# Attention and two MLPs on one core: operand differences issued ahead of their halves, six weight sums taken from the converted words, and the first block's inputs on ScalarE's DMA queue

## The chip, the cores and the metric

The kernel runs on one core of one Trainium2 chip. The metric is the device time of one execution in microseconds (us). The kernel before takes 918.45 us, the median of 3 runs (918.18 to 919.23). The engines are named PE (TensorE), DVE (VectorE), ACT (ScalarE), POOL (GpSimd) and SP (SyncE, which before the change issues every transfer).

## The reference

Attention with a causal window of 128 and a linear bias, then two MLPs with squared ReLU, all in float32:

```python
# q, k, v: 4 batches, 8 heads, 576 positions, 64 columns
scores = np.where(mask, scale * np.matmul(q, k.transpose(0, 1, 3, 2)) + bias[None], -1000000000.0)
attn = softmax(scores)                      # mask: 0 <= i - j < 128
x = matmul(attn, v)                         # as 2304 tokens x 512
x = (s * np.maximum(x @ w_in1, 0.0) ** 2 + b) @ w_out1
out = np.maximum(x @ w_in2, 0.0) ** 2 @ w_out2
# w_in: 512 x 2048, w_out: 2048 x 512
```

## The kernel before, in words

**Accuracy.** Every operand of a float32 product is split into a high and a low half of a shorter type, and each product is the sum of three: high by high, high by low, low by high. A split is two instructions: ACT copies the operand into the short type (the high half), and DVE subtracts that from the operand (the low half). The low half therefore waits for ACT, on DVE.

**Fewer products.** Both MLPs multiply blocks of 2 by 2 in seven products instead of eight. That needs sums and differences of blocks: of the weights (done once, kept in DRAM as halves and loaded where they are needed), of the inputs (`difference`, L957, then `halve_input`, L984), and in the second MLP's second layer of the activations.

**Weights.** They arrive as 64-bit words that are converted on ACT, DVE and POOL. For the second MLP's `w_out` the pair k has words in tiles `raws[(k, r)]`, r = 2 and 3. Before, the converted words of these two rows of blocks are stored to DRAM (`store_words`, tokens `x`) and loaded again later (`load_words`, tokens `y`, into new tiles r = 4 and 5), and from those `second_sums` (tokens `N`, two for each pair) makes four combinations, `second_sum_halves` (`R`) splits them, and `store_second_sums` (`t`) writes them to DRAM (L872 to L940). Pairs 0 and 1 use other buffers, the eight pairs are otherwise alike.

**Order.** The whole program is a list of some 2,460 tokens in one string, `ORDER` (L37 on). Each token calls one function of a table (L1220 for the steps of the last stage), and the class `InOrder` (L19) keeps every engine's instructions in the order in which the functions issue them. All rows of the profile therefore have line L29. Two more tables say which engine takes an instruction that several could take (`UNIT_ENGINES`, `CHOICE`: `N1.1:v` puts that sum on DVE, without an entry it goes to POOL).

**Stages.** From 0 to about 400 us attention and the first MLP run interleaved, in units of 256 positions. The last 64 positions of each sequence are the *tail*: eight small units (`tail_unit`, L450 on), whose last step, `places`, copies an attention output with ACT and writes it to DRAM (`xd` in the profile). The first block of the second MLP starts with `load_input` (L943): four tiles `yf`, two transfers each, from these writes; the differences `t1s`, `yt` and two in place; the halves `m2xh`, `m2xl` and so on. While this happens PE finishes the last groups of the first MLP, whose operands are `ga_62h`, `ga_62l`, `ga_63h`, `ga_63l` and whose products are in `oa`.

The second MLP has four blocks of tokens, n = 0 to 3. For n = 0 and 1 first and second layer are interleaved. For n = 2 and 3 the first layer's results of all eight pairs are kept in SBUF, and the second layer is done product by product: for each of the kinds m = 1, 2, 7, 6, 5, 4, 3, and for each pair, a weight is loaded (token `e`, `load_second`), the operand is made (`g`, `second_operand`, L1044), and nine matmuls follow (`X`, `second_product`, into `q`). The operand of m = 7 is a difference of two results, put into `r_all`; that of m = 6 takes two instructions, that of m = 3 one, and the other kinds use a result as it is:

```python
if m == 7:
    tt(src, a11, a21, ALU.subtract)
elif m == 6:
    tt(a21, a21, a22, ALU.add)
    tt(a11, a21, a11, ALU.subtract)
elif m == 3:
    tt(a12, a12, a11, ALU.subtract)
split(*operand_halves(n, e), src, act_copy, dve_sub)
```

So on DVE the difference and the low half of the same operand stand next to each other, with ACT's copy between them in time.

Of the kernel before, what the change touches and what calls it, by code (L numbers as in the profile page):

```python
# [11 lines left out]
U32 = mybir.dt.uint32  # L12
# [3 lines left out]
P = 128  # L16


class InOrder:  # L19
# [24 lines left out]
    H13 c21 L15 c20 M12 c22 C10 U10 G14 a23 H14 X10 l30 G15 M13 L16 S11 M14 b23 L17 G16 P11 D13 L18 T11 H15 c23 M15 H16
    C11 G17 l32 a30 G18 U11 H17 X11 H18 L19 G19 b30 L20 S12 M16 L21 k0.1 a32 l31 M17 M18 P12 T12 a31 H19 G20 c30 C12 H20
    L22 l33 G21 b32 U12 X12 L23 G22 H21 S13 L24 M19 a33 b31 M20 M21 H22 P13 l34 b33 T13 G23 C13 c31 a34 M22 H23 U13 L25
    c33 G24 G25 c32 L26 k3.0 D14 L27 H24 M23 H25 X13 D15 S14 G26 G27 M24 l35 b34 L28 L29 P14 k4.1 T14 M25 H26 a35 C14
    H27 c34 k4.0 G29 b35 U14 M26 D16 X14 G28 H28 S15 L30 c35 P15 M27 M28 T15 C15 D17 G30 L31 H29 G31 U15 X15 L32 S16 M29
    H30 H31 D18 G32 L33 P16 T16 M30 D19 C16 H32 G33 M31 M32 H33 S17 U16 L34 P17 T17 X16 G34 C17 M33 L35 H34 S18 U17 M34
    G35 X17 H35 P18 L36 D20 T18 G36 C18 M35 D21 S19 U18 L37 H36 P19 T19 X18 M36 C19 S20 D22 U19 G37 L38 H37 P20 M37 T20  # L50
    G38 X19 C20 L39 S21 U20 H38 G39 H39 L40 P21 M38 G40 L41 M39 D23 H40 T21 G41 L42 X20 H41 C21 k6.0 S22 U21 M40 k0.0
    P22 T22 X21 C22 M41 S23 U22 G42 D24 H42 k7.0 k1.1 L43 P23 T23 X22 M42 C23 S24 G43 H43 k3.1 U23 P24 L44 T24 D25 D26
    C24 X23 M43 k1.0 G44 H44 L45 G45 S25 U24 L46 D27 M44 k5.0 X24 P25 T25 H45 G46 k2.1 C25 H46 D28 L47 n0.0 n0.1 S26 U25
# [1218 lines left out]
```

## Time and profile before

| | |
|---|---|
| median of 3 runs | 918.45 us (918.18 to 919.23) |
| the profiled execution | 916.52 us, its span 914.7 us |
| PE busy | 878.5 us, 96% of the span |
| DVE busy | 663.4 us, 73% |
| ACT busy | 536.7 us, 59% |
| POOL busy | 167.7 us, 18% |
| transfers | 216.83 MB, mean 237 GB/s |
| chain of work that ended last | PE 81%, DVE 9%, ACT 4%, DMA 3% |

The span is the time from the first instruction to the last. The profiled execution is one more execution, 1.9 us below the median of the others. A share of busy time is an average over stages that differ much, so the table says only that PE is the engine that is nearly always at work; where it is not, the windows and the waits tell.

### The profile page before, as it was taken

Reading aid. Unit: us, or ns where it says so; the run is one execution under the profiler, and the core shown is the slowest. Engines: PE = TensorE matmul, PEld = TensorE weight load, DVE = VectorE, ACT = ScalarE, POOL = GpSimd, SP = SyncE. Lnnn points to the kernel's source line nnn. Section 1 sums busy time; section 2 is a strip of 40 time slices with the busy share of each in tenths; the row PEclk is TensorE's granted clock in tenths of the full one; section 3 lists DMA queues with packets and bytes.
Section 4 is the critical chain, followed back from the end, with each engine's and each line's share of the span. In section 5 each row is a group of like instructions: output and inputs, shape, how many; then the busy total and the mean of one; then the engine's idle time right before and its main releaser. Section 6 shows DMA issues by size and latency. Waiting matters only on the chain.

```text
span 914.7 us, 16299 instructions
## 1 busy us (share of the span) xinstructions
PE 878.5 (96%) x5680; PEld 787.4 (86%) x5680; DVE 663.4 (73%) x1504; ACT 536.7 (59%) x1227; POOL 167.7 (18%) x242
## 2 busy tenths in 40 slices
PE   5899999999999999989999999999999989999988
PEld 3789998878777777769999998888999989999988
DVE  7998885554558788865565866897969968448775
ACT  7888776454546677754454555666655635446442
POOL 4333221000024454200200122222213200000000
PEclk9899999999999999999999999999999999999999
DMA  9553636126337978988679766887999987876683
GB/s 344 174 190 99 201 112 195 47 70 219 103 100 242 313 248 271 307 305 316 226 287 355 262 229 198 306 294 261 319 336 349 327 282 252 292 265 229 187 271 98
DMA packets 131378, 216.83 MB, mean 237 GB/s; under 512 B 15840, under 2 KB 74208, under 8 KB 131296
## 3 DMA queue, kind: packets, MB, share of 16 engines
q1 hardware_dynamic: 131296, 215.79, 70.0%
q8 instruction: 45, 0.74, 0.3%
q14 instruction: 37, 0.30, 0.1%
HBM read 146.02 MB, written 69.73 MB: 236 GB/s over the span
## 4 chain that ended last, share of the span: by engine, by line
PE 81%; DVE 9%; ACT 4%; DMA 3%; issue 2%; SPq 1%; POOL 0%; ACTq 0%; DVEq 0%
PE ha L29 14%; PE po L29 14%; PE px L29 13%; PE oa L29 12%; PE py L29 10%; PE q L29 8%; PE s L29 7%; PE u L29 2%; DMA m2wol<-wd 1%; DVE ywoh L29 1%; DVE st L29 1%; DVE m2woh L29 1%; DVE pr_t L29 1%; DMA yf<-xd 1%; DMA st<-w_out 1%
## 5 line engine op out<-in xcount | busy, mean ns | idle before, releaser
L29 POOL TENSOR_TENSOR st<-st 128x256 int32<-128x256 int32 (+1 forms) x123 | 87.2, 729 | 363.8 <-DVE st L29 251.0
L29 ACT ACTIVATE pr<-pr,nd 128x256 f32<-128x256 f32 (+1 forms) x125 | 57.9, 474 | 49.5 <-DVE nd L29 49.5
L29 ACT ACTIVATE st<-st 128x512 int32<-128x512 uint32 (+3 forms) x74 | 62.4, 859 | 5.6 <-DVE st L29 3.4
L29 DVE SCALAR_TENSOR_TENSOR r_all<-r_all,s_sb 128x256 f32<-128x256 f32 (+1 forms) x64 | 43.0, 675 | 24.4 <-ACT r_all L29 23.8
L29 ACT ACTIVATE tr<-tr 128x384 f32<-128x384 f32 x48 | 25.2, 525 | 55.4 <-DVE tr L29 55.3
L29 PE MATMUL oa<-ga,woh 128*128 128x256 f32 x256 | 48.2, 287 | 0.0
L29 ACT ACTIVATE r_all<-ha 128x256 f32<-128x256 f32 (+1 forms) x64 | 31.0, 486 | 24.7 <-PE ha L29 19.2
L29 DVE SCALAR_TENSOR_TENSOR st<-st 128x512 int32<-128x512 int32 (+1 forms) x42 | 37.3, 890 | 11.0 <-ACT st L29 10.4
L29 PEld LDWEIGHTS oa<-ga,woh 128*128 128x128 f32 x256 | 39.7, 191 | 2.2 <-issue 1.8
L29 DVE CUSTOM_DVE_ANT_0 pr<-s,bases 128x256 f32<-128x256 f32 (+1 forms) x96 | 31.7, 385 | 11.3 <-PE s L29 11.3
L29 PE MATMUL ha<-x0h,wih 128*128 128x256 f32 x128 | 38.4, 300 | 0.0
L29 PE MATMUL ha<-x0l,wih 128*128 128x256 f32 x128 | 36.6, 286 | 0.0
L29 PE MATMUL ha<-x0h,wil 128*128 128x256 f32 x128 | 36.6, 286 | 0.0
L29 PE MATMUL oa<-ga,wol 128*128 128x256 f32 x128 | 36.2, 283 | 0.0
L29 POOL TENSOR_TENSOR sph<-wih,wil 128x256 f32<-128x256 f32 x17 | 13.5, 814 | 117.7 <-PE ha L29 117.2
L29 ACT ACTIVATE r_all<-px 128x384 f32<-128x384 f32 x32 | 15.7, 490 | 29.5 <-PE px L29 29.4
L29 PE MATMUL s<-raw 64*128 64x256 f32 (+1 forms) x224 | 30.5, 388 | 0.8 <-DVE x0l L29 0.8
L29 DVE TENSOR_SCALAR st<-st 128x512 int32<-128x512 int32 (+2 forms) x52 | 26.2, 507 | 5.9 <-ACT st L29 5.1
L29 POOL TENSOR_TENSOR sph<-sph 128x256 f32<-128x256 f32 x26 | 22.6, 888 | 33.7 <-DVE spl L29 20.9
L29 PE MATMUL px<-m2xl,m2wil 128*128 128x384 f32 x138 | 27.9, 337 | 0.0
L29 PEld LDWEIGHTS ha<-x0h,wih 128*128 128x128 f32 x128 | 24.9, 195 | 3.5 <-issue 2.5
L29 PE MATMUL ha<-x2h,wih 128*128 128x512 f32 x64 | 26.4, 412 | 0.0
(681 smaller groups left out, 2765.9 us busy)
## 6 DMA issues: line engine op xcount, KB each, us to landing
m2wih<-wd SPq DMA_DIRECT2D x19, 512.0 KB, 6.5
st<-w_in SPq DMA_DIRECT2D x8, 1024.0 KB, 6.0
st<-w_out SPq DMA_DIRECT2D x16, 512.0 KB, 5.0
ws<-spl SPq DMA_DIRECT2D x16, 512.0 KB, 4.2
m2wih<-ws SPq DMA_DIRECT2D x16, 512.0 KB, 6.1
wd<-m2wol SPq DMA_DIRECT2D x14, 512.0 KB, 4.5
m2wol<-we SPq DMA_DIRECT2D x26, 256.0 KB, 4.4
st<-w_out SPq DMA_DIRECT2D x6, 1024.0 KB, 6.9
```

The lines of the kernel that those rows point to most:

```text
L29: ins = op(*args, **kw)
```

## The change

Four things change.

1. `second_operand` is cut in two. `second_difference` (token `q`) has the subtractions of m = 7, 6 and 3, and stands in `ORDER` ahead of the token `g`, which now only splits. For m = 7 the differences go alternately into two buffers (`r_all` and `tu`).
2. For the pairs 2, 3 and 4 (`AT_ONCE`) the second sums are made from the converted words' own tiles; `ORDER` has no `x` and `y` for them any more, which is 6 stores and 6 loads of 256 KB, and their `N`, `R` and `t` stand earlier.
3. The eight writes of the tail's results, and the eight transfers of `load_input` for the first block, are issued by ACT instead of SP.
4. `ORDER`, `UNIT_ENGINES` and `CHOICE` are new as a whole. The built program has the same 5,248 matmuls; DVE has 1,524 instructions instead of 1,506, POOL 232 instead of 247, ACT 1,080 activations instead of 1,082 and 16 transfers, SP 690 transfers instead of 718. Of the sums of 128x256, POOL has 15 fewer and DVE 17 more.

```diff
...
-    X3.41 X3.42 X3.43 g3.48 X3.44 e3.45 e3.51 e3.48 X3.45 X3.46 O3.5.2 g3.49 X3.48.2 g3.47 X3.49.2 X3.50.2 X3.51.2
...
+    X3.39 e3.48 e3.45 X3.40 X3.41 X3.42 e3.54 X3.43 e3.47 X3.44 X3.45 g3.48 e3.51 e3.55 q3.51 e3.53 O3.5.2 q3.53 g3.46
...
-    N1.1:v N2.1:v N3.0:v N3.1:v N7.1:v S0.1:g S1.1:g S2.0:g S3.0:g S3.1:g S4.0:g b0.0:vg b2.2:vg b3.0:vg b3.1:vg
...
+    N0.1:v N1.0:v N3.0:v N4.0:v N4.1:v N5.1:v N6.1:v S0.0:g S0.1:g S1.0:g S1.1:g S3.1:g b0.0:vg b0.2:vg b2.0:vg
...
-EARLY, SOONER = 3, 2
+EARLY, SOONER, AT_ONCE = 3, 2, (2, 3, 4)
...
-            sync.dma_start(x_dram[LAST][:, 2 * hq:2 * hq + 2, cols], y.rearrange("p (y t) -> p y t", y=2))
+            scalar.dma_start(x_dram[LAST][:, 2 * hq:2 * hq + 2, cols], y.rearrange("p (y t) -> p y t", y=2))
...
-        return raws[(k, r)][:, h * DM:(h + 1) * DM]
+        return raws[(k, r - 2 if r > 3 and k in AT_ONCE else r)][:, h * DM:(h + 1) * DM]
...
     def load_input(n, q):
+        queue = sync if n else scalar
...
-            sync.dma_start(y[:, :, :BLK], a0[:, c, :])
-            sync.dma_start(y[:, :, BLK:], a1[:, c, :P])
+            queue.dma_start(y[:, :, :BLK], a0[:, c, :])
+            queue.dma_start(y[:, :, BLK:], a1[:, c, :P])
...
-    def second_operand(n, e):
+    def parts_of(n, e):
         m, y = SECOND[e // NP], e % NP
         a11, a22, a12, a21 = (result_of(n * NP + y, c) for c in range(4))
+        return m, a11, a22, a12, a21, {1: a11, 2: a12, 7: temp(f"u{3 + y % 2}"), 6: a11, 5: a21, 4: a22, 3: a12}[m]
+
+    def second_difference(n, e):
+        m, a11, a22, a12, a21, src = parts_of(n, e)
         tt = vector.tensor_tensor
-        src = {1: a11, 2: a12, 7: temp("u3"), 6: a11, 5: a21, 4: a22, 3: a12}[m]
         if m == 7:
             tt(src, a11, a21, ALU.subtract)
         elif m == 6:
...
         elif m == 3:
             tt(a12, a12, a11, ALU.subtract)
-        split(*operand_halves(n, e), src, act_copy, dve_sub)
+
+    def second_operand(n, e):
+        split(*operand_halves(n, e), parts_of(n, e)[-1], act_copy, dve_sub)
...
```

**The order on DVE in the last stage (n = 3), kinds m7 and m6.** `r_all` (and `tu` after the change) is the difference of an m7 operand, a tile that begins with `m2w` the half that is made from it; `yw..` are the first layer's results. Before:

```order
L29 TENSOR_TENSOR r_all<-ywol_7370 128x384
L29 TENSOR_TENSOR m2wil_4703<-r_all,m2wil_4703 128x384
L29 TENSOR_TENSOR ob_9148<-q_8982,k3m 128x512
L29 TENSOR_TENSOR ob_9154<-q_8983,k3m 128x256
L29 TENSOR_TENSOR r_all<-ywol_7370,ywoh_7518 128x384
L29 TENSOR_TENSOR m2wil_4703<-r_all,m2wil_4703 128x384
```

After the change:

```order
L29 TENSOR_TENSOR tu_7116<-ywol_7372 128x384
L29 TENSOR_TENSOR ywoh_7222<-ywoh_7222,ywil_7115 128x384
L29 TENSOR_TENSOR ywil_7115<-ywoh_7222,ywil_7115 128x384
L29 TENSOR_TENSOR m2wil_4702<-tu_7116,m2wil_4702 128x384
L29 TENSOR_TENSOR m2woh_4723<-ywih_7029,m2woh_4723 128x384
L29 TENSOR_TENSOR r_all<-ywol_7372,ywoh_7512 128x384
L29 TENSOR_TENSOR tu_7116<-ywoh_7512,yr_7643 128x384
L29 TENSOR_TENSOR m2wih_4481<-ywoh_7222,m2wih_4481 128x384
```

Between a difference and the half made from it now stand two or more other instructions.

**The order on ACT where the first MLP ends and the second MLP's first inputs come.** `raw_t` is a tail unit's output, `xd` where it is written, `yf` an input tile, `ga_62h` and `ga_63h` the operands of the last groups. Before:

```order
L29 ACTIVATE raw_t_4346<-u_t_4553 128x128
L29 ACTIVATE spl<-sph 128x2x256
L29 ACTIVATE ga_62h<-r_all,s_sb 128x512
L29 ACTIVATE spl<-sph 128x2x256
L29 ACTIVATE r_all<-ha_63_4577 128x512
L29 ACTIVATE m2xh_4638<-yf_4571 128x768
L29 ACTIVATE ga_63h<-r_all,s_sb 128x512
```

After the change:

```order
L29 DMA xd_118<-raw_t_4363 128x2x64
L29 DMA yf_4587<-xd_118 128x2x256
L29 DMA yf_4587<-xd_116 128x2x128
L29 DMA yf_4590<-xd_116 128x2x128
L29 DMA yf_4590<-xd_117 128x2x256
L29 DMA yf_4605<-xd_116 128x2x128
L29 DMA yf_4605<-xd_117 128x2x256
L29 ACTIVATE ga_62h<-r_all,s_sb 128x512
L29 DMA yf_4612<-xd_118 128x2x256
L29 DMA yf_4612<-xd_116 128x2x128
L29 ACTIVATE spl<-sph 128x2x256 x2
L29 ACTIVATE r_all<-ha_63_4574 128x512
```

One write and six loads stand ahead of `ga_62h`, two loads behind it; `m2xh` and `ga_63h` follow the copy of `ha_63` as before.

**The order on DVE at the same place.** `t1s` is the first difference of the inputs. Before:

```order
L29 TENSOR_TENSOR m2xh_4638<-yf_4571,m2xh_4638 128x768
L29 TENSOR_TENSOR t1s<-yf_4574,yf_4571 128x768
L29 SCALAR_TENSOR_TENSOR ga_63l<-r_all,s_sb,ga_63h 128x512
L29 TENSOR_TENSOR yt_4647<-yf_4592,t1s 128x768
L29 TENSOR_TENSOR m2wih_4650<-t1s,m2wih_4650 128x768
```

After the change:

```order
L29 TENSOR_TENSOR m2xh_4629<-yf_4587,m2xh_4629 128x768
L29 SCALAR_TENSOR_TENSOR ga_63l<-r_all,s_sb,ga_63h 128x512
L29 TENSOR_TENSOR t1s<-yf_4590,yf_4587 128x768
L29 TENSOR_TENSOR yt_4638<-yf_4605,t1s 128x768
L29 TENSOR_TENSOR yf_4590<-yf_4605,yf_4590 128x768
```

`ga_63l` now stands ahead of `t1s`.

## Rows read from the trace of the kernel before

**Rows 1.** The page, part 1: busy time of each engine, share, instructions.
```profile
PE 878.5 (96%) x5680; PEld 787.4 (86%) x5680; DVE 663.4 (73%) x1504; ACT 536.7 (59%) x1227; POOL 167.7 (18%) x242
```

**Rows 2.** Windows: length, busy of PE, PEld, DVE, ACT, POOL; clock, DMA, GB/s.
```profile
0.00:60.00 60.00, 43.40 (x361) 35.98 (x362) 51.80 (x154) 50.62 (x118) 24.59 (x47) 0.94 0.67 233
...
340.00:420.00 80.00, 74.31 (x464) 60.71 (x463) 63.04 (x161) 54.10 (x132) 17.12 (x31) 1.00 0.88 298
420.00:690.00 270.00, 269.40 (x1441) 247.94 (x1441) 193.74 (x347) 150.85 (x302) 49.38 (x64) 1.00 0.81 284
...
740.00:770.00 30.00, 26.51 (x195) 24.38 (x194) 21.78 (x43) 12.24 (x27) 0.00 (x0) 1.00 0.77 258
...
860.00:884.00 24.00, 20.57 (x159) 19.23 (x159) 17.63 (x36) 7.44 (x16) 0.00 (x0) 1.00 0.62 200
```

**Rows 3.** Waits of PE, 690 to the end: us, times, longest.
```profile
PE q L29 <- ACT m2woh L29: 2.3, 2, 1.5
PE q L29 <- ACT m2wil L29: 2.0, 3, 0.9
PE q L29 <- ACT m2wih L29: 1.8, 1, 1.8
PE py L29 <- DVE ywol L29: 0.8, 1, 0.8
...
PE q L29 <- DMA m2wol<-wd: 0.8, 1, 0.8
```

**Rows 4.** Timeline of DVE, 862 to 884: start, length, instruction, idle before and releaser.
```profile
862.86 1.14 DVE L29 TENSOR_TENSOR ywih<-ywih 128x384 f32<-128x384 f32 x2
...
867.42 0.55 DVE L29 TENSOR_TENSOR r_all<-ywol 128x384 f32<-128x384 f32 x1
868.57 0.56 DVE L29 TENSOR_TENSOR m2wil<-r_all,m2wil 128x384 fp32r<-128x384 f32 x1 [0.59 <-ACT m2wil L29]
```

**Rows 5.** Timeline of PE, 862 to 884.
```profile
866.33 1.24 PE L29 MATMUL q<-m2wih,m2wil 128*128 128x256 f32 x9
867.41 1.24 PE L29 MATMUL q<-m2wil,m2wih 128*128 128x256 f32 x9
...
871.13 1.69 PE L29 MATMUL q<-m2xl,m2wil 128*128 128x256 f32 x9 [0.85 <-ACT m2wil L29]
```

**Rows 6.** Timeline of ACT, 386 to 411.
```profile
390.63 0.71 ACT L29 ACTIVATE ga_62h<-r_all,s_sb 128x512 fp32r<-128x512 f32 x1
391.24 0.62 ACT L29 ACTIVATE spl<-sph 128x512 fp32r<-128x512 f32 x1
392.87 0.60 ACT L29 ACTIVATE r_all<-ha 128x512 f32<-128x512 f32 x1 [1.01 <-PE ha L29]
396.45 0.85 ACT L29 ACTIVATE m2xh<-yf 128x768 fp32r<-128x768 f32 x1 [2.98 <-DMA yf<-xd]
397.20 0.71 ACT L29 ACTIVATE ga_63h<-r_all,s_sb 128x512 fp32r<-128x512 f32 x1
```

**Rows 7.** Timeline of SP's DMA queue, 386 to 411.
```profile
390.23 0.37 SPq L29 DMA_DIRECT2D xd<-raw_t  x1
392.99 2.94 SPq L29 DMA_DIRECT2D yf<-xd  x6
```

**Rows 8.** Waits of PE, 340 to 420.
```profile
PE oa L29 <- DVE ga_63l L29: 2.3, 1, 2.3
```

**Rows 9.** Timeline of DVE, 386 to 411.
```profile
399.14 0.96 DVE L29 TENSOR_TENSOR t1s<-yf,yf 128x768 f32<-128x768 f32 x1 [0.85 <-DMA yf<-xd]
400.01 0.75 DVE L29 SCALAR_TENSOR_TENSOR ga_63l<-r_all,s_sb,ga_63h 128x512 fp32r<-128x512 f32 x1
```

**Rows 10.** Groups by form: busy, mean ns of one, idle before.
```profile
L29 POOL TENSOR_TENSOR st<-st,st 128x256 f32<-128x256 f32 x19 | 18.9, 1014 | 10.5 <-DMA st<-wx 10.2
L29 DVE TENSOR_TENSOR st<-st,st 128x256 f32<-128x256 f32 x17 | 7.3, 455 | 1.3 <-POOL st L29 0.6 <-DMA st<-wx 0.4
```

**Rows 11.** Waits of PE, 0 to 60.
```profile
PE s L29 <- DVE f_0wih L29: 1.4, 2, 1.2
```

More of the change, by code (lines that the diff above doesn't have):

```diff
@@ L44 @@
[L44 to L53, printed above, removed]
@@ new lines @@
+    T2.1 a5.3 b5.3 p13.6 j12.3 p13.2 h12.1 u13 x5.3 r12.3 F11.2 c5.5 F11.6 W63 p13.7 a6.1 h12.2 F12.3 b6.1 a6.0 F12.4
+    t3.3 h12.3 d5.4 v13 F11.11 F12.5 b6.0 j13.0 F12.11 F12.0 S6.0 p13.4 Y2.2 F12.10 S6.1 j13.2 F12.1 r13.2 c6.2 l6.2
+    p13.5 c6.0 c6.3 p14.1 d5.5 d3.1 F12.9 d5.0 a6.2 b6.2 m14 j13.1 r13.1 c6.1 F12.6 c6.4 F11.8 p13.3 F12.7 h13.2 F12.2
+    h13.1 j13.3 p14.6 T2.3 r13.0 r13.3 p14.2 l6.3 Y3.1 F12.8 u14 p14.7 x6.2 a6.3 h13.0 l7.0 F13.1 T2.2 b6.3 F13.2 d4.4
+    F13.0 v14 a7.0 F13.6 j14.0 b7.0 p14.4 F13.4 r14.0 l7.1 h13.3 a7.1 F13.7 p14.5 c6.5 F13.8 x6.3 F13.5 b7.1 F13.10
@@ new lines @@
+    X2.19 e2.23 q2.22 X2.20 C2.1.1 e2.33 r23.3 C2.1.0 e2.32 X2.21 O2.2.2 q2.23 e2.27 g2.25 e2.30 e2.28 e2.35 e2.34
+    O2.2.0 m24 X2.24 g2.23 e2.29 g2.22 e2.31 X2.25 q2.26 q2.28 p24.2 X2.22 g2.26 X2.23 g2.27 X2.26 g2.28 C2.7.1 q2.30
+    g2.32 X2.27 q2.29 X2.28 e2.42 X2.32 g2.33 e2.40 g2.30 X2.33 e2.46 g2.29 e2.41 q2.31 g2.34 e2.37 q2.49 C2.7.0 e2.36
+    X2.29 e2.39 X2.30 g2.31 g2.35 X2.34 g2.38 X2.31 e2.38 g2.40 g2.39 g2.36 X2.40 g2.37 X2.35 p24.6 q2.48 V3.5 w27.0
+    e2.43 q2.50 X2.36 X2.37 X2.38 e2.48 e2.54 g2.41 g2.42 e2.47 q2.52 e2.49 g2.43 e2.51 e2.44 q2.54 X2.39 g2.44 X2.41
@@ L147 @@
+    g3.53 X3.46 O3.5.0 X3.47 g3.51 q3.54 g3.49 g3.50 X3.48.0 g3.54 X3.49.0 g3.55 O3.4.2 X3.50.0 X3.51.0 X3.52.0 X3.53.0
+    X3.54.0 X3.55.0 X3.48.2 X3.49.2 O3.3.0 X3.48.1 X3.50.2 X3.51.2 X3.52.2 X3.53.2 X3.49.1 O3.4.0 X3.54.2 X3.55.2
+    X3.50.1 X3.51.1 X3.52.1 X3.53.1 X3.54.1 O3.3.2 X3.55.1 O3.3.1
 """
-UNIT_ENGINES = """vvvvss vvvvvs svvvsv vvvvss vvvvvv vvvvss vvvvsv svvvss vvvvss vvvvss vvvvss vvvvss svvvss ssvvvv svvvss vsvsvv vvvvvs vvvvsv svvvvv vvssvv vvsvvs ssssvs vssvsv vsvsvs ssvvsv sssvss vsvsss vvsvvv vvvvvs vvsvsv vvsvss vvsvss""".split()
+UNIT_ENGINES = """vvvvss vvvvss vvsvvs vvvvsv vvvvvv vvvvss vvvvsv svvvss vvvvss vvvvss vvvvss svvvvv vssvsv vvvvss vssvsv vsvsvv svvvvv vsvssv vsvsss svvvvv svvvsv sssvss vvssss svvvvs svvvsv ssvvsv vsvssv vssvsv vsvsss vssvss vvssss vvvvss""".split()
@@ L161 @@
+    b7.0:vg b7.3:vg c34:g c35:g n0.1:v n0.3:v n0.4:v n1.0:v n1.5:v n2.0:v n2.2:v n3.2:v n3.3:v n4.0:v n4.1:v n4.2:v
+    n4.3:v n4.5:v n5.0:v n5.2:v n5.3:v n5.5:v n6.0:v n6.1:v n6.2:v n6.5:v n7.2:v n7.4:v n7.5:v
 """.split())
 PIECE_ENGINES = [x.split() for x in ("sv sv sv sv", "sv sv sv sv", "sv sv sv sv", "sv sv sv sv sv sv")]
-EARLY, SOONER = 3, 2
+EARLY, SOONER, AT_ONCE = 3, 2, (2, 3, 4)
 EVICT_ENGINES = "svsv svsv ss".split()
@@ L950, in load_input @@
         if t == 0:
-            sync.dma_start(y[:, :, :BLK], a0[:, c, :])
-            sync.dma_start(y[:, :, BLK:], a1[:, c, :P])
-        else:
-            sync.dma_start(y[:, :, :P], a1[:, c, P:])
-            sync.dma_start(y[:, :, P:], a2[:, c, :])
+            queue.dma_start(y[:, :, :BLK], a0[:, c, :])
+            queue.dma_start(y[:, :, BLK:], a1[:, c, :P])
+        else:
+            queue.dma_start(y[:, :, :P], a1[:, c, P:])
+            queue.dma_start(y[:, :, P:], a2[:, c, :])
     def difference(n, i):
@@ L1219, in attention_mlp2_kernel @@
         for e in range(7 * NP):
-            table.update({f"{x}{n}.{e}": lambda y=y, n=n, e=e: y(n, e) for x, y in (("e", load_second), ("g", second_operand), ("X", second_product))})
+            table.update({f"{x}{n}.{e}": lambda y=y, n=n, e=e: y(n, e) for x, y in (("e", load_second), ("q", second_difference), ("g", second_operand), ("X", second_product))})
             for t in range(3):
```

196 lines of the change are left out of this document (97 added, 99 removed).

## The prediction

> **What bounds the kernel now.** I read four kinds of view, from the whole to single instructions. The page first: TensorE (PE) is busy 878.5 us, 96% of the span of 914.7 [rows 1]. Nothing that only makes another engine faster, or takes transfers away, can show unless PE waits for it, so I look for the places where PE waits. The table by windows gives them: PE has no idle time to speak of from 420 to 690 (269.40 of 270), and loses 16.6 us in the first 60 us, 5.7 between 340 and 420, 3.5 between 740 and 770 and 3.4 between 860 and 884 [rows 2]. The change touches all four, and the long middle.
>
> The waits of PE in the last stage (690 to the end) name ScalarE (ACT) first: 2.3, 2.0 and 1.8 us, six waits, all of a `q` product for an operand's high half [rows 3]. The DVE timeline of 862 to 884 shows why. A product of kind m7 takes a difference on DVE (867.42, 0.55 us), then ACT copies it, then DVE takes the low half (868.57 to 869.13); before that DVE stands still for 0.59 us, because difference and low half are neighbours in its order and the ACT copy lies between them [rows 4]. That chain lasts 869.13 - 867.42 = 1.71 us; with two differences (kind m6), which take 1.14 us together, it is 0.6 longer. PE needs 867.41 - 866.33 = 1.08 us for the nine matmuls of a product [rows 5]. So wherever such products stand together, DVE's idle time sets the pace. PE shows it twice: it waits, and some of its products are stretched to 1.69 us where others take 1.24 [rows 5]. Eight in the two windows are so stretched, 8 x 0.45 = 3.6 us.
>
> **The change, part by part.** *Differences as own steps.* The number of subtractions stays; the order moves them ahead by a few instructions, so that ACT's copy runs while DVE does something else. What can go is DVE's stall, and with it PE's waits. I take exactly the six waits: 2.3 + 2.0 + 1.8 = **-6.1 us** [rows 3]. Bounds: 0, if another link of the chain sets the same pace; and -10.5, if all of PE's idle time in the two windows and the stretch go (3.5 + 3.4 + 3.6) [rows 2, 5]. I take the value between: were both windows as short as PE's busy time in them (20.57 and 26.51), DVE's 17.63 and 21.78 us would fill them to 86% and 82% [rows 2], which leaves room for the waits to close and little for the stretch. The second buffer for m7 (before, every m7 went through `r_all`) is needed for this and costs nothing: no instruction is added. Late next is DVE itself, with a wait on `ywol`, and a load (`m2wol`, 0.8) [rows 3].
>
> *Inputs of the first block on ACT's queue.* Here a wait is added. Before, SP issued the last tail write at 390.23, waited for it, and at 392.99 began the input loads: 2.76 us of waiting and 2.94/6 = 0.49 for each load [rows 7]. ACT meanwhile did `ga_62h` at 390.63 [rows 6]. Now ACT issues that write itself, and six loads that depend on it stand in its order ahead of `ga_62h`, two more behind it. Behind the wait are queued: `ga_62h`, two `spl` copies, the copy of `ha_63`, `m2xh`, `ga_63h`. At SP's prices ACT is free at 390.23 + 2.76 + 6 x 0.49 = 395.93, so `ga_62h` ends at 396.64 instead of 391.34. Two more loads (0.98), two copies (0.62 each, overlapping by 0.1), the copy of `ha_63` (0.60), `m2xh` and `ga_63h` (0.85 + 0.71) [rows 6] put the end of `ga_63h` near 400.9, and DVE's `ga_63l` (0.75) near 401.7. Who waits for that is PE: `oa` already waits 2.3 us for `ga_63l` [rows 8], which before ended at 400.01 + 0.75 = 400.76 [rows 9]. That is **+0.9 us**. The other side: the new order also puts `ga_63l` ahead of `t1s` on DVE (order in the section on the change), and `t1s` had itself waited 0.85 for a load and taken 0.96 [rows 9]. If issuing on ACT cost next to nothing, `ga_63l` would follow `ga_63h` at about 398.0 and end near 398.7: -2.1. I take +0.9, because the only row of an issue is SP's, and keep -2.1 as an end. The seven other tail writes, 0.37 each at most by SP's row [rows 7], lie where ACT is busy 54.10 us of 80 [rows 2]: nothing.
>
> The Trainium skill (DMA: Bandwidth & Descriptors, "Issuing engines are not separate DMA queues") says that all issuers' transfers run on the same 16 engines, and that another issuer only saves the sequencer's time to start them, which is usually small against the transfer. That speaks against any faster landing here; the row of SP shows 0.49 an issue, not small. By the 50 ns that the same page gives for a sequencer's dispatch ("Anatomy of one DMA", there for GpSimd's path), an estimate, the eight loads would hold ACT for 0.4 us, and the term would be about -1.7 instead of +0.9; no row here shows it.
>
> *Sums straight from the words.* Six stores and six loads of 256 KB go. In the last stage and the middle, PE's only named wait for a load is 0.8 us, on another tile [rows 3]: 0, between -0.8 and +1. *Sums moved between engines.* POOL's list is 15 sums shorter, DVE's 17 longer; by the rows a sum is 1.01 us on POOL and 0.46 on DVE [rows 10]. So DVE gets 17 x 0.46 = 7.8 us more. In 420 to 690, where most of them stand, DVE is busy 193.74 of 270 and PE does not wait [rows 2]: 0. If that cover were gone, it would cost at most those 7.8. *The re-ordered start and attention.* PE waits there for first loads and conversions that the change does not shorten; the row I can name is a DVE one of 1.4 us [rows 11]. 0, with 1.4 to either side, and as much for the order from 340 to 420.
>
> **Sum.** -6.1 + 0.9 = -5.2. The profiled execution took 916.52, so it would take 911.3. It lies 1.9 below the median of the runs, and I put the same difference on the median: 918.45 - 5.2 = **913.2 us**.
>
> **The rivals.** *A. The stall only moves.* The differences run ahead but the low halves, loads or DVE's own order then hold PE just as long. For it: DVE's 0.55 us an instruction, at three or four a product, is 1.6 to 2.2 against PE's 1.08; that is what a row of m7 and m6 products together needs. Against it: between 860 and 884 DVE is idle over a quarter of the time [rows 2]. Time: 918.45 + 0.9 = 919.3, no measurable change. This is also what one would see if the split steps ended up next to each other again; the printed order says that they mostly do not.
>
> *B. ACT's queue becomes the bound between 340 and 420 (slower).* ACT works in order, and now holds 2.76 + 8 x 0.49 = 6.7 us of waiting and issuing for the inputs and 8 x (0.37 + some 0.2 for its own copy) = 4.6 for the writes, 11.3 in all [rows 7]. For it: in this window PE already waits for what ACT feeds. Against it: ACT has 26 us idle there [rows 2]. If all 11.3 reached PE, the time would be 918.45 - 6.1 + 11.3 = 923.6. It is slower than before by more than can be measured from the point where over 7.9 of the 11.3 come through.
>
> *C. Issues on ACT are nearly free.* Then the order of `ga_63l` before `t1s` gains: 918.45 - 6.1 - 2.1 = 910.3. For it: nothing in the trace of before, in which ACT issues no transfer. Against it: SP's rows.
>
> **How the numbers follow.** About 0.2% (1.8 us) is what a measurement of this kernel can tell from no change. The forecast has a chance of 0.48, C 0.22, A 0.17, B 0.13. Faster by over 0.2% (below 916.6): the forecast and C, 0.70. Within: A but for a small part, 0.15. Slower (above 920.3): B and that part of A, 0.15. The range reaches from 907 (between -10.5 + 0.9, which is 908.9, and -10.5 - 2.1, 905.9) to 920, which takes in A and leaves B out.
>
> **What would show it.** Right: in the last stage the six waits for ACT are gone, DVE's idle time of 0.59 between a difference and its low half too, and the m7 and m6 products last 1.24 and not 1.69. At the transition: ACT idle about 2.8 us ahead of its loads, and `oa` waiting 2 to 4 us for `ga_63l`. PE in the middle still idle under 1 us. Wrong: waits of the same sum on `ywol` or DVE's low halves in the last stage (A), PE waiting over 10 us between 340 and 420 (B), or new waits on second-layer weights in the middle.

## The result and the profile after

The changed kernel takes 905.45 us (median of 4 runs, 904.09 to 907.78) against 918.32 us for the kernel before in the same comparison (4 runs): a ratio of 0.9861, 95% interval 0.9835 to 0.9887, or 12.9 us. The prediction was 913.2 with a range of 907 to 920; the time lies below the range. The profiled execution has a span of 902.4 us against 914.7.

The page of the changed kernel, part 1 (busy time of each engine, share, instructions), answers to [rows 1]:

```profile
PE 877.9 (97%) x5680; PEld 791.0 (88%) x5680; DVE 661.5 (73%) x1522; ACT 531.4 (59%) x1225; POOL 152.0 (17%) x227
```

PE's busy time is the same within 0.6 us. What went is idle time: 914.7 - 878.5 = 36.2 us before, 902.4 - 877.9 = 24.5 after. The table by windows of the changed kernel (columns as in [rows 2]) shows where:

```profile
0.00:60.00 60.00, 47.24 (x362) 39.66 (x363) 52.48 (x154) 51.09 (x119) 24.31 (x47) 0.91 0.66 233
...
340.00:420.00 80.00, 73.06 (x445) 58.87 (x444) 60.89 (x150) 51.15 (x122) 16.07 (x29) 0.98 0.89 304
420.00:690.00 270.00, 270.00 (x1451) 249.08 (x1450) 199.68 (x368) 150.09 (x306) 44.24 (x60) 1.00 0.80 276
...
740.00:770.00 30.00, 30.00 (x245) 30.00 (x244) 26.37 (x53) 17.57 (x37) 0.00 (x0) 1.00 0.87 290
...
860.00:884.00 24.00, 24.00 (x203) 24.00 (x202) 19.62 (x42) 11.62 (x26) 0.00 (x0) 1.00 0.88 287
```

The windows at 740 and 860 are full now (26.51 of 30 and 20.57 of 24 before [rows 2]), and the list of PE's waits from 690 to the end, six and more before [rows 3], is empty. DVE gets through 42 instructions in 24 us instead of 36. From 340 to 420 PE is idle a little longer than before, and its clock was granted 0.98 instead of 1.00.

The timeline of DVE in the changed kernel shows the distance between a difference (`tu<-ywol`) and its low half (`m2wil<-tu`), to be held against the stall of 0.59 us in [rows 4]:

```profile
854.18 0.55 DVE L29 TENSOR_TENSOR tu<-ywol 128x384 f32<-128x384 f32 x1
854.64 0.55 DVE L29 TENSOR_TENSOR ywoh<-ywoh,ywil 128x384 f32<-128x384 f32 x1
855.23 0.56 DVE L29 TENSOR_TENSOR ywil<-ywoh,ywil 128x384 f32<-128x384 f32 x1
855.71 0.55 DVE L29 TENSOR_TENSOR m2wil<-tu,m2wil 128x384 fp32r<-128x384 f32 x1
```

DVE does not stop between them: one instruction starts every 0.46 to 0.59 us. The products that were stretched to 1.69 us [rows 5] take 1.24 now, as the prediction said:

```profile
866.35 1.24 PE L29 MATMUL q<-m2xl,m2wih 128*128 128x256 f32 x9
867.43 1.24 PE L29 MATMUL q<-m2wih,m2wil 128*128 128x256 f32 x9
```

Windows of time do not compare two kernels well, because the work shifts. So the time that PE lost is also counted by place in PE's own work, which both kernels have in the same amount. This table is worked out from the starts of the matmuls: from each start to the next, less the steady interval of its shape (0.228 us for 512 columns, 0.174 for 384, 0.120 for 256), summed over stretches of PE's work (us of it, 887 in all). Left out are the stretches from 60 to 340, where no kernel differs by over 0.5 from the one before, and from 440 to 520, where those shown lose 0.3 or 0.4.

| us of PE's work | 0-60 | 340-440 | 520-600 | 600-680 | 680-720 | 720-780 | 780 to end |
|---|---|---|---|---|---|---|---|
| before | 10.7 | 8.2 | 2.0 | 0.6 | 3.3 | 6.1 | 5.2 |
| changed | 10.7 | 11.2 | 0.7 | 0.7 | 0.2 | -0.1 | -0.1 |
| changed, again | 13.9 | 10.2 | 0.6 | 0.7 | -0.1 | -0.1 | -0.1 |
| a_sync | 11.1 | 6.2 | 0.7 | 0.7 | 0.3 | -0.1 | -0.1 |
| a_sync_again | 11.3 | 9.1 | 0.6 | 0.6 | -0.1 | 0.0 | -0.1 |
| a_inputs_sync | 11.7 | 7.0 | 0.6 | 0.7 | 0.0 | -0.1 | -0.1 |
| a_q_adjacent | 11.9 | 10.4 | 0.6 | 0.6 | -0.1 | 14.6 | 11.7 |
| b_split2 | 10.5 | 8.7 | 1.0 | 0.6 | 2.9 | 3.0 | 5.2 |
| b_split2_out | 11.1 | 7.4 | 2.3 | 0.6 | 3.4 | 0.6 | 1.4 |
| b_stage3 | 11.7 | 6.7 | 2.6 | 0.6 | 3.2 | 4.2 | 8.1 |
| b_words | 10.8 | 7.0 | 13.1 | 0.6 | 0.5 | 7.0 | 5.6 |
| a_words2 | 13.4 | 10.2 | 2.2 | 13.4 | 11.6 | 4.0 | -0.1 |

From before to changed: +3.0 where the first MLP ends, -1.3 and -3.1 in the second MLP's first three blocks, -6.2 and -5.3 in the two last blocks, where the operand differences are. The last two are the prediction's subject; the others are not what it said.

### The profile page after: what moved, and what is told of

It reads as the page before. It is cut to its first block, busy times and chain, and to the rows that moved or that the text cites. A ratio compares the mean times of both kernels' runs of the same rounds, so it can differ in the third digit from the quotient of the medians.

```text
span 902.4 us, 16274 instructions
## 1 busy us (share of the span) xinstructions
PE 877.9 (97%) x5680; PEld 791.0 (88%) x5680; DVE 661.5 (73%) x1522; ACT 531.4 (59%) x1225; POOL 152.0 (17%) x227
## 4 chain that ended last, share of the span: by engine, by line
PE 84%; DVE 7%; ACT 4%; DMA 2%; issue 2%; POOL 0%; ACTq 0%; DVEq 0%; SPq 0%
PE po L29 15%; PE px L29 14%; PE ha L29 12%; PE q L29 12%; PE oa L29 12%; PE py L29 11%; PE s L29 6%; PE u L29 1%; DVE pr_t L29 1%; ACT st L29 1%; DMA yf<-xd 1%; DMA wx<-ewil 1%; DVE st L29 1%; DVE f_0wih L29 1%; ACT f_3woh L29 0%
## 5 line engine op out<-in xcount | busy, mean ns | idle before, releaser
L29 POOL TENSOR_TENSOR st<-st 128x256 int32<-128x256 int32 (+1 forms) x118 | 82.9, 724 | 356.4 <-DVE st L29 232.2
L29 ACT ACTIVATE st<-st 128x512 int32<-128x512 uint32 (+3 forms) x67 | 57.7, 868 | 3.1 <-DVE st L29 3.0
L29 DVE SCALAR_TENSOR_TENSOR r_all<-r_all,s_sb 128x256 f32<-128x256 f32 (+1 forms) x64 | 41.0, 645 | 23.3 <-ACT r_all L29 23.1
L29 PE MATMUL oa<-ga,wol 128*128 128x256 f32 x128 | 36.2, 282 | 0.0
L29 DVE TENSOR_SCALAR st<-st 128x512 int32<-128x512 int32 (+3 forms) x59 | 29.1, 493 | 5.9 <-ACT st L29 4.8
L29 ACT ACTIVATE r_all<-px 128x384 f32<-128x384 f32 x32 | 15.6, 486 | 24.7 <-PE px L29 24.5
L29 PEld LDWEIGHTS s<-raw 64*128 64x128 f32 x224 | 18.4, 191 | 9.3 <-issue 4.6
L29 PE MATMUL ha<-x1h,wih 128*128 128x512 f32 x64 | 26.5, 414 | 0.0
```

Source lines behind the costliest of these rows:

```text
L29: ins = op(*args, **kw)
```

## The experiments

Names that begin with a are edits of the changed kernel, those with b edits of the kernel before. Each ratio is to the kernel before, timed beside it; the changed kernel's is 0.9861.

### Distance alone, order alone: a_q_adjacent and b_split2

`a_q_adjacent` puts all 48 differences back in front of their own splits:

```diff
-    t7.2 q2.17 X2.9 q2.16 e2.14 g2.13 q2.24 g2.12
...
-    e2.18 e2.16 j23.2 X2.11 X2.12 r23.2 g2.17 R7.3 R7.0 g2.16
+    t7.2 X2.9 e2.14 g2.13 g2.12
...
+    e2.18 e2.16 j23.2 X2.11 X2.12 r23.2 q2.17 g2.17 R7.3 R7.0 q2.16 g2.16
```

> The changed kernel with every difference put back directly ahead of its own split (48 of them), all else as in the changed kernel. Theory 1 (the gain of the last stage comes from the distance between a difference and its low half): PE's waits for ACT come back in the stretches with kinds m7 and m6, and the time rises by about what the kernel before lost there, 5.2 + 1.0 us from 740 to 780 and 4.2 + 1.0 from 860 to 900, so 905.5 + 8 to 12 = 914 to 917 us. Rival 1 (the gain comes from the new order of loads, sums and products as a whole): 905 to 908 us, no waits for ACT.

Measured: 934.4 us, ratio 1.0184 (1.0156 to 1.0212). That is 30 us above the changed kernel by the ratios, three times what was expected, and slower than the kernel before. PE loses 14.6 + 11.7 us where the changed kernel loses nothing. Its DVE timeline has the stall back:

```profile
865.79 0.55 DVE L29 TENSOR_TENSOR r_all<-ywil,ywoh 128x384 f32<-128x384 f32 x1
866.93 0.56 DVE L29 TENSOR_TENSOR m2wil<-r_all,m2wil 128x384 fp32r<-128x384 f32 x1 [0.59 <-ACT m2wil L29]
...
867.88 0.55 DVE L29 TENSOR_TENSOR tu<-ywoh,ywoh 128x384 f32<-128x384 f32 x1
869.02 0.56 DVE L29 TENSOR_TENSOR m2wil<-tu,m2wil 128x384 fp32r<-128x384 f32 x1 [0.59 <-ACT m2wil L29]
```

Counted in the traces from 720 us on, a low half on DVE stands directly behind the instruction that made its operand, and waits there for ACT, 49 times in `a_q_adjacent` (31 us of DVE), 50 times in the kernel before (33 us), 3 times in `b_split2` (5 us) and never in the changed kernel. So in the new order the distance is necessary. It is not so that the new order gains by itself; without the distance it is the worse of the two orders. The excess over what was expected is not all direct stall: three stretches at half clock behind waits (see the last section) hold some 4.4 of the 26.3 us, an estimate from the starts of the matmuls, and one wait of PE for ACT's `k3m` 4.0.

`b_split2` is the converse: the kernel before, its order kept, with the differences moved ahead past the two operand steps before them.

The change in the kernel (the last line in words):

```diff
+    def second_difference(n, e):
...
-        split(*operand_halves(n, e), src, act_copy, dve_sub)
+    def second_operand(n, e):
+        split(*operand_halves(n, e), parts_of(n, e)[-1], act_copy, dve_sub)
...
+    q2.e and q3.e (48 tokens), each ahead of the second g before its own g
```

> The kernel before with the difference as an own step, moved ahead past the two operand steps before it (where another value in the same buffer allows), all else as in the kernel before, its order too. Theory 1: the six waits for ACT in the last stage go, 918.3 - 8 to 11 = 907 to 910 us. Rival 1: at most 2 us gained, 916 to 918 us, because loads and the order of the other instructions set the pace.

Measured: 911.36 us, ratio 0.9936 (0.9921 to 0.9951), 5.8 us faster, between the two expectations. In the trace PE's loss in the block n = 2 falls from 6.1 to 3.0, in the last block it stays at 5.2; the rest of the gain is not in these blocks. That the time fell by nearly the 6.1 us of the prediction's first term is therefore luck and bears nothing out: 3.1 us of it stand where the term was read. The waits of PE from 770 on in `b_split2`:

```profile
PE q L29 <- DMA m2wol<-we: 1.3, 1, 1.3
PE q L29 <- DVE m2woh L29: 1.2, 1, 1.2
PE q L29 <- DMA m2wih<-we: 0.3, 1, 0.3
```

The waits for ACT are gone, and PE waits 1.6 us for weights and 1.2 for a half that DVE makes: the distance is not sufficient. The 1.3 us wait has a second price behind it: the granted clock is 0.50 from 875.4 to 878.9, where 18 matmuls of 256 columns take 3.89 us instead of some 2.3.

```profile
875.39 3.89 PE L29 MATMUL q<-m2wol,m2wil 128*128 128x256 f32 x18 [1.33 <-DMA m2wol<-we]
```

### What the order adds: SP's queue (b_split2_out, b_stage3, b_split2_loads)

Why are the weights late? The timeline of SP's queue in the kernel before, from 859 to 873:

```profile
860.22 0.43 SPq L29 DMA_DIRECT2D m2wil<-we  x1
869.75 3.09 SPq L29 DMA_DIRECT2D out<-ob  x5
872.94 0.40 SPq L29 DMA_DIRECT2D m2wol<-we  x1
```

SP issues nothing for 9 us, because the next transfer in its order is an output store, and that waits for DVE's sum `ob` (9.3 us in the list of SP's waits). The loads of the next weights stand behind it, and then the five stores of one token take another 3.1 us. Whether those loads could have started sooner, their places being free, these rows do not show. `b_split2_out` takes these stores (kinds m2 and m5) off SP's queue and changes nothing else in `b_split2`:

```diff
-            write_out(n, ..., ob[:, u * BLK:(u + 1) * BLK])
+            write_out(n, ..., ob[:, u * BLK:(u + 1) * BLK], gpsimd if m in (2, 5) else sync)
...
-            sync.dma_start(out[rows:rows + size, c], ob[a * size:(a + 1) * size])
+            (queue or sync).dma_start(out[rows:rows + size, c], ob[a * size:(a + 1) * size])
```

> b_split2 (the kernel before with the differences two operands ahead) with one more edit: the output stores of the kinds m2 and m5 in the last stage are issued by GpSimd instead of SP. Theory 5 (once the differences are ahead, what holds PE between 860 and 880 is SP's queue: an output store waits for DVE's sum, and the loads of the next weights stand behind it): PE's waits on m2wih and m2wol loaded from we after 860 go, and 3 to 5 us of the 5.3 us that PE loses there; a ratio of 0.988 to 0.990 to the kernel before. Rival 5 (the loads wait for their places, which the order of the products frees late): within 1 us of b_split2, a ratio of 0.9925 to 0.9945.

Measured: 910.14 us, ratio 0.9918 (0.9887 to 0.9949); it missed the expected 0.988 to 0.990, and its runs lie 6 us apart, so the time does not show a gain over `b_split2`. The trace of one execution of each does, at the place: PE's loss falls from 5.2 to 1.4 in the last block and from 3.0 to 0.6 in the block before, and of the waits of PE from 850 to 900 one is left, and it is not for a weight:

```profile
PE q L29 <- DVE m2woh L29: 1.2, 1, 1.2
```

So distance (6.1 to 3.0 in the first of the two blocks) and loads that do not stand behind a waiting store (5.2 to 1.4 and 3.0 to 0.6) together account for 11.3 - 2.0 = 9.3 of the 11.3 us in these two executions. They are the fastest of four of `b_split2_out` (907.0) and the slowest of four of `b_split2` (912.2), so the second part may be smaller elsewhere. The changed kernel seems to get the second part without another queue; this is read from its timeline and has no run of its own. In its order the output store goes in at 863.12, and weights are issued right before and behind it.

```profile
862.59 0.43 SPq L29 DMA_DIRECT2D m2wih<-we  x1
863.12 0.38 SPq L29 DMA_DIRECT2D out<-ob  x1
863.54 0.43 SPq L29 DMA_DIRECT2D m2wil<-we  x1
864.07 2.46 SPq L29 DMA_DIRECT2D out<-ob  x4
```

`b_stage3` puts the whole last block of the changed kernel, in its order, into `b_split2` (the edit in words):

```diff
-    all e3, q3, g3, X3, C3, O3 tokens in the order of b_split2
+    the same tokens in the order of the changed kernel, hung to the same products
```

> b_split2 with the loads, differences, operands, products, copies and outputs of the last block (n = 3) in the order of the changed kernel; all else, the block n = 2 included, as in b_split2. Theory 6 (in the last block distance and order are both needed: the old order with distance loses 5.3 us, the new order without distance 14.6, the two together nothing): PE loses under 0.5 us after 770, 5 us less than b_split2, a ratio near 0.988. Rival 6 (the last block of the changed kernel runs without waits because of what comes before it): PE still loses 2 to 5 us there, 0.991 to 0.994.

Measured: 914.81 us, ratio 0.9971 (0.9957 to 0.9986). Its results come out different from the other kernels', probably because in this mixed order a value is overwritten before its last use, which no run shows; the instructions are the same. The stretch of PE's work from 840 on, where the kernel before lost 5.2 us, loses 0.0; but 8.1 us are lost earlier, from 800 to 840, where the new steps of the last block follow the old ones of the block before: `px` waits 3.4 us on issue and 1.3 on `tu`, and the clock is 0.50 for 6.8 us from 831.3, some 2.3 us more by the starts of the matmuls. Theory 6 holds for the place it was made for and fails for the total: here the order of one block could not be moved without that of its neighbour.

`b_split2_loads` moves 72 loads of second weights ahead by up to six products instead (the edit in words):

```diff
-    e2.16 to e2.55 and e3.16 to e3.47 where b_split2 has them
+    each up to six X ahead, not ahead of the last X that reads its place
```

> The kernel before with the differences as own steps two operands ahead (b_split2), and in addition the loads of second weights of the kinds m7, m6, m5, m4 and m3 in the last stage moved ahead by up to six products, where their place is free and their data are written; nothing else. Theory 4 (with the differences ahead, SP's queue sets the pace: loads stand behind output stores that wait for DVE): the waits of 1.3 to 2.2 us on m2wih and m2wol, loaded from we, go, and the time falls by 4 to 7 us below b_split2, to a ratio of 0.986 to 0.989 to the kernel before. Rival 4 (the place of a weight is not free any sooner, or the transfers themselves are late): within 1 us of b_split2, 0.9925 to 0.9945.

Measured: 932.29 us, ratio 1.0154 (1.0131 to 1.0178). Moved that far, the loads themselves wait at the head of SP's queue for the writes of the data that they read (6.0 us for `we<-m2xl`, 4.1 for `we<-m2wih`, 2.8 for `we<-m2wol` between 735 and 760), and PE waits 6.7 us for one of them. The expectation took these data as written; they were not. The run says nothing for or against theory 4, only that "earlier" in an ordered queue is not "sooner".

### The queue of ACT (a_sync, a_inputs_sync, best1, best3)

ACT's timeline in the changed kernel where the first MLP ends:

```profile
390.17 0.41 ACTq L29 DMA_DIRECT2D xd<-raw_t  x1
394.30 3.23 ACTq L29 DMA_DIRECT2D yf<-xd  x6
397.57 0.72 ACT L29 ACTIVATE ga_62h<-r_all,s_sb 128x512 fp32r<-128x512 f32 x1 [7.43 <-DMA yf<-xd]
```

An issue takes 3.23/6 = 0.54 us of ACT, about as on SP (0.49 [rows 7]), and from the tail's write to the first load 4.1 us pass instead of 2.8. `ga_62h` comes at 397.57 instead of 390.63 [rows 6]. What waits on PE is the product with `ga_62h`, 2.9 us, not `ga_63l` as before [rows 8]:

```profile
PE oa L29 <- ACT ga_62h L29: 2.9, 1, 2.9
...
PE oa L29 <- DVE ga_63l L29: 0.3, 1, 0.3
```

These figures differ between executions. In a second profile of the same kernel (`after_again`) 2.87 us pass ahead of the loads, `ga_62h` comes at 399.27, and PE waits half as long for it:

```profile
393.26 0.37 ACTq L29 DMA_DIRECT2D xd<-raw_t  x1
396.13 3.09 ACTq L29 DMA_DIRECT2D yf<-xd  x6
...
PE oa L29 <- ACT ga_62h L29: 1.5, 1, 1.5
```

`a_sync` puts these transfers back on SP:

```diff
-            scalar.dma_start(x_dram[LAST][:, 2 * hq:2 * hq + 2, cols], ...)
+            sync.dma_start(x_dram[LAST][:, 2 * hq:2 * hq + 2, cols], ...)
...
-        queue = sync if n else scalar
+        queue = sync
```

> The changed kernel with the tail's writes and the first block's inputs issued by SP again, the order of all tokens unchanged. Theory 2 (ACT's queue costs the 3.1 us by which the first block's first product starts later than before): ga_62h is no longer behind the loads, the first product of the first block starts about 3 us sooner, 905.5 - 3 = 902.5 us. Rival 2 (the loss comes from the new order there, not from the queue): 904.5 to 906.5 us.

Measured: 899.93 us, ratio 0.9819 (0.9802 to 0.9835). The same kernel again, and beside it the changed kernel again:

> The changed kernel with both groups of transfers on SP, again, beside the changed kernel itself. Theory 2 (a wait of PE of 2.9 us, and matmuls at half clock after it, both caused by ga_62h standing behind the loads on ACT): 4 to 5 us below after_again, a ratio of 0.981 to 0.982. Rival 2 (the difference between the earlier calls was the chip's): within 2 us of after_again.

> The changed kernel, unaltered, beside a_sync_again and a_words2 on one chip. Theory 2: a ratio of 0.986 to the kernel before, and 4 to 5 us above a_sync_again.

Measured: 902.37 us (0.9827, 0.9807 to 0.9848) and 905.86 us (0.9875, 0.9856 to 0.9894), 3.5 us apart, less than the 4 to 5 expected. So this part of the change costs some 3.5 us, and the changed kernel without it is the fastest version that was found. By place the traces are less clear: `a_sync` lies 5.0 us below the changed kernel from 340 to 440 (11.2 to 6.2), `a_sync_again` only 1.1 below `after_again` (10.2 to 9.1), and in that second pair 2.6 of the 4.0 us stand in the first 60 us, where the edit does nothing.

`a_inputs_sync` leaves the eight tail writes on ACT and puts only the inputs back (the second of the two edits above).

> The changed kernel with only the first block's inputs issued by SP again; the tail's eight writes stay on ACT's queue. Theory 2a (the wait and the issues for the inputs, ahead of ga_62h, cost it all): a ratio to the kernel before within 0.001 of that with both on SP (0.982), some 4 us below the changed kernel. Rival 2b (the writes on ACT, each behind its own copy, take their part): halfway, a ratio of 0.984, with PE waiting longer for pr_t and ACT copies between 360 and 395 than with both on SP.

Measured: 901.13 us, ratio 0.9817 (0.9797 to 0.9838), the same as with both, within an interval of 0.002 on either side: the inputs cost it all as far as these runs can tell, as theory 2a has it. The runs of the three kernels with the inputs on SP lie between 899.2 and 902.7 us, the eight of the changed kernel between 904.1 and 907.8.

Two attempts to gain more at this place failed. Both start from `a_sync`:

```diff
-    L63 Y0.0 Y0.1 M61 Y0.3 H62 Y0.2 w0.0 n7.5 w0.1 f7.0 f7.1 G63 w0.3 V0.1 H63
+    L63 w0.0 w0.1 Y0.0 Y0.1 M61 Y0.3 H62 Y0.2 n7.5 f7.0 f7.1 G63 H63 w0.3 V0.1   (best1)
+    L63 Y0.0 Y0.2 w0.0 w0.1 Y0.1 Y0.3 M61 H62 n7.5 f7.0 f7.1 G63 w0.3 V0.1 H63 V0.2   (best3)
```

> The changed kernel with both groups of transfers on SP (as a_sync), the operand step of group 63 directly behind its square (ahead of the first input's copy m2xh, which waits for a load), and the first two weights of the first block loaded ahead of its inputs instead of behind them. Theory 2 extended: PE's waits of 0.5 for ga_63l and 1.3 for m2wol go, the first block starts 1 to 2 us sooner than in a_sync: a ratio of 0.980 to 0.981. Rival: m2xl, the last input, then holds PE as long: 0.982, with a wait of py on m2xl of over 1 us.

> The changed kernel with both groups of transfers on SP (as a_sync), the four input tiles loaded in the order in which they are needed (first, third, then the first two weights, then second and fourth), and the third tile's halves made ahead of the differences. If the weight m2wol and then m2xl are what holds PE after the last product of the first MLP, the first block's first product starts 1 to 2 us sooner and the ratio is 0.980 to 0.981. If the differences (which now come later) hold it instead: 0.982 to 0.984, with waits of px on m2wol or m2wih made from yt or t1s.

Measured: 904.41 us (0.9849, 0.9826 to 0.9872) and 906.92 us (0.9885, 0.9867 to 0.9903), both slower than `a_sync` and above what was expected. In `best1` the waits for `ga_63l` and the weight go, and `py` waits 2.2 and 1.2 us on `m2xl` instead, the rival's wait and longer than it said; in `best3` the wait for the weight goes, one of 4.4 us for ACT's `tm` comes, and the 0.5 for `ga_63l` stays.

### Sums straight from the words (b_words, a_words, a_words2)

`b_words` makes this part alone in the kernel before (in words behind the first line; the list that says which engine takes which of the second sums, `CHOICE`, changes with it):

```diff
-EARLY, SOONER = 3, 2
+EARLY, SOONER, AT_ONCE = 3, 2, (2, 3, 4)
...
-    x2.2 to x4.3, y2.4 to y4.5; N, R, t of pairs 2 to 4 behind F15
+    N, R, t of pairs 2 to 4 at the products where the changed kernel has them; l4.1 behind N3.1, l5.0 behind R4.1
```

> The kernel before with the second sums of pairs 2, 3 and 4 taken straight from the converted words, at the places that the changed kernel gives them (sums, halves and stores), without the six stores and six loads of words; two loads of words stand behind the last use of their buffer. All else as before. Theory 3 (this part of the change gives the gain between 560 and 740, by taking work and transfers out of the crowded stretch before the last stage): 3 to 4 us faster, a ratio near 0.996, and the waits of py on ywoh and ywol near 700 are gone. Rival 3: within 1 us of the kernel before.

Measured: 924.85 us, ratio 1.0081 (1.0062 to 1.0101), 7.8 us slower than the kernel before beside it. At the place of theory 3, from 680 to 720 of PE's work, the loss falls from 3.3 to 0.5, and the waits on `ywoh` and `ywol` are gone. But PE comes to this stretch 10 us later here, so DVE had that time too, and the run does not separate the two. And 11.1 us come in between 520 and 600, most of them at one spot, a wait of PE of 7.4 us for ACT's `tr` with some 2.3 us at half clock behind it; 1.3 more are lost in the two last blocks. The waits on `ywoh` in the kernel before and on `tr` in `b_words`, and ACT's timeline there:

```profile
PE py L29 <- DVE ywoh L29: 0.8, 1, 0.8
...
PE px L29 <- ACT tr L29: 7.6, 2, 7.4
...
586.77 1.22 ACT L29 ACTIVATE st<-st 128x512 int32<-128x512 uint32 x2 [3.92 <-DMA st<-w_in]
587.89 0.47 ACT L29 ACTIVATE tr<-px 128x384 f32<-128x384 f32 x1
```

`tr` stands in ACT's order behind the conversion of the next words, and these had not arrived. Their buffer `st` is one of three, and the words from which the sums are made hold it longer now; so the six stores and loads had, as I read it, bought free buffers.

`a_words` and `a_words2` undo this part in the changed kernel, and give the second sums the engines of the kernel before (`CHOICE`). In `a_words` the stores of words stand directly behind their conversion, in `a_words2` directly ahead of the load that needs the buffer (the last line in words):

```diff
-EARLY, SOONER, AT_ONCE = 3, 2, (2, 3, 4)
+EARLY, SOONER, AT_ONCE = 3, 2, ()
...
+    x2.2 to x4.3 and y2.4 to y4.5 back; y, N, R, t of all pairs at the products where the kernel before has them
```

> The changed kernel with the second sums of all pairs, their halves and their stores where the kernel before has them, and the six stores and six loads of words back (no pair works from the converted words). Theory 3 (the 3 to 4 us gained between 560 and 740 come from the sums that now stand earlier and the transfers that are gone): 905.5 + 3 to 4.5 = 908.5 to 910 us, with waits of PE on DVE's results and on loads between 690 and 740. Rival 3 (they come from the new order of everything else): 905 to 907 us.

> The changed kernel with no sums straight from the words: the six stores of words stand directly ahead of the next load into the same buffer, the six loads, all second sums, their halves and their stores where the kernel before has them. Theory 3 (the gain between 560 and 740 comes from these sums standing earlier): 2.5 to 5 us above after_again, with waits of PE between 690 and 740 on ywoh, ywol or loads. Rival 3 (it comes from the new order of everything else): within 1 us of after_again, no such waits.

Measured: 957.7 us (1.0437, 1.0416 to 1.0458) and 935.08 us (1.0196, 1.0178 to 1.0213). The first is spoilt by SP's queue, which stood still ahead of `wx<-st` for 10 us twice:

```profile
467.57 0.32 SPq L29 DMA_DIRECT2D m2woh<-ws  x1
477.24 0.32 SPq L29 DMA_DIRECT2D wx<-st  x1
```

The second has no such stop before 600 (2.2 us lost from 520 to 600), and loses 13.4 us from 600 to 680 and 11.6 from 680 to 720, to waits of this kind (waits of PE from 640 to 780):

```profile
PE py L29 <- DVE ywih L29: 3.9, 1, 3.9
PE py L29 <- DVE ywoh L29: 2.7, 2, 1.9
PE q L29 <- DVE m2wih L29: 2.1, 1, 2.1
PE py L29 <- DVE ywol L29: 1.9, 1, 1.9
```

2.5 to 5 us above the changed kernel were expected of `a_words2`; 29 came. That this part of the change matters here is what both directions show: 3.3 to 0.5 from 680 to 720 in `b_words`, 0.9 to 25.0 from 600 to 720 in `a_words2`. Neither separates the place of the sums from the six stores and loads or from the choice of engines. The size of 25 belongs to the new order, which fills the place of the late sums with other work; it is not what this part is worth in the change.

## Why the prediction was wrong

**The reading of what bounds the kernel held.** The idle time stood where [rows 2] has it, PE's work did not change, and the gain is all idle time of PE.

**The first term was too small, and its mechanism only part of the matter.** The step that failed is "I take exactly the six waits", -6.1 us. The two blocks lost 6.1 + 5.2 = 11.3 us by place in PE's work, and all of it went: -11.5, beyond the end that the prediction kept (-10.5). The six waits are what the view lists; the stretched products and shorter pauses are nearly as much again. The prediction named the stretch (3.6 us) and argued that DVE at 86% leaves little room for it. DVE ran in the window at 19.62 of 24, 82%, with PE full: there was room. The mechanism of the prediction is necessary (`a_q_adjacent`), but as it was described, with the old order kept (`b_split2`), it takes 3.1 of the 11.3 us; there rival A was the better account, with its "loads" as the new wait. What held PE besides was SP's queue, where loads of weights stood behind an output store that waited: with both out of the way 9.3 of the 11.3 us went (`b_split2_out`). That the new order removes the second by the place of its stores is read from one timeline. I had read the order of DVE and ACT and not that of SP in this stage, though SP's silence from 860.65 to 869.75 was in the trace.

**The second term was too small by 1 to 2.** +0.9 was forecast, +3.0 (2.0 in the second profile) came. The issue price taken from SP's row was right (0.54 and 0.52 us on ACT against 0.49), and so rival C, issues that cost nearly nothing, is out. PE waited for `ga_62h` first, an operand that was ready early before, and not 2 to 4 us for `ga_63l`, so the old wait for `ga_63l` could not be reused as cover; and ACT stood 4.1 us, in the second profile 2.9, ahead of its loads, where 2.8 was forecast. Still the waits alone add only 1.3 and 0.1 us to what the kernel before lost here. The term that was missing is the clock: 1.7 and 1.9 us were lost in all matmuls at half clock behind the wait (the window below holds 1.4 of the 1.7), and none in the kernel before. The gain from `ga_63l` ahead of `t1s` is in this sum and could not be seen apart.

The Trainium skill (DMA: Bandwidth & Descriptors, "Issuing engines are not separate DMA queues") calls the sequencer's time to start a transfer usually small relative to the transfer. Here six such starts took 3.23 us of ACT's order, ahead of an operand. The prediction's other estimate, 0.4 us of ACT for all eight, was ten times too low.

**The middle was not 0.** From 520 to 720 PE lost 4.4 us less than before, where the prediction's sum has nothing. The two waits on `ywoh` and `ywol`, 0.8 us each, looked too small to matter and had no term of their own. With what follows them they are 3.3 us, and they go in `b_words`, with the reservations made there. My bound of -0.8 looked only at the wait for a transfer; the sums that stood with the transfers on DVE and ACT may be the greater part, which no run separates. Of the 1.3 us gained from 520 to 600 no experiment tells the cause.

**Sums moved to DVE cost nothing**, as forecast: PE is busy 270.00 of 270 from 420 to 690 with DVE at 199.68 instead of 193.74. The start was 0 in the first profile and 3.2 worse in the second, whose execution was 2 us longer.

**Rival B** had the right place: the queue of ACT costs some 3.5 us there. But only 2 to 3 of its 11.3 us reached PE.

## What to carry to other kernels

Where an operand is a difference and then a copy on another engine and a subtraction, put other work between them, and then look at the next ordered queue: here all of the gain came only when the loads did not stand after a store that waits (3.1 of 11.3 us came without). Read the idle time of PE by place in its own work, not from the list of waits alone: the six waits for ACT held 6.1 of the 11.3 us. A transfer's issue on a compute engine is an instruction in its order, with its wait; eight of them belong behind the operand that PE needs next, or on a queue with nothing behind them.

## What was not expected of the hardware

After a wait of PE of 2.9 us (behind one of 2.3 us the kernel before kept 1.00) the granted clock fell to one half, 1.2 instead of 2.4 GHz, and stayed there for about 3 us. The windows of the changed kernel around the wait for `ga_62h`:

```profile
392.00:395.00 3.00, 3.00 (x15) 2.49 (x14) 0.00 (x0) 0.00 (x0) 0.00 (x0) 1.00 0.81 280
395.30:398.30 3.00, 0.18 (x1) 0.00 (x0) 0.00 (x0) 0.72 (x1) 0.00 (x0) 1.00 0.64 187
398.34:399.10 0.76, 0.49 (x1) 0.19 (x1) 0.76 (x2) 0.00 (x0) 0.00 (x0) 0.98 0.91 277
399.13:402.20 3.07, 3.07 (x7) 2.48 (x8) 2.38 (x5) 2.37 (x4) 0.00 (x0) 0.50 0.91 293
```

In these 3.07 us matmuls of 512 columns started 0.43 us apart instead of 0.23, so seven of them lost 1.4 us on top of the wait.

The length of the pause alone does not tell when this happens. The clock went to 0.50 behind this wait of 2.9 us, and in other traces behind waits of 4.4 (`best3`), 2.7 (`a_sync_again`, 0.50 from 406 to 409), 2.2 (`a_q_adjacent`), 2.1 and 1.3 (`b_split2`), and 1.5 us (`after_again`, a mean of 0.72 from 400 to 406). It stayed at 1.00 behind waits of 2.3 (before), 1.8 (`a_inputs_sync`) and 1.3 us (`a_sync`). The row of `after_again`:

```profile
400.00:406.00 6.00, 5.33 (x13) 3.31 (x13) 4.71 (x8) 3.09 (x5) 0.00 (x0) 0.72 0.92 319
```

The profiled execution of `a_sync_again`, with its wait at half clock, took 902.4 us; of four other runs two took 900.1 and two 902.6 and 902.7. They have no trace, so that the clock makes this difference is not shown. For a sum like the prediction's, such a pause can have a second price behind it, some 1.3 to 2.3 us in these runs, and these runs do not tell when it is due.
